# The order of the steady batches written anew in a fused attention and feed-forward kernel

## The chip, the cores and the metric

The kernel runs on one core of a Trainium2 chip. The metric is device time in microseconds (us) from one launch to its end; a time is the median of several runs, and beside it stands one profiled execution, from which all rows of the trace come.

## What is computed

For each of 8 batches and 8 heads (576 tokens, 64 columns), a softmax of phi over 32 memories weights the keys and values into 32 memory rows; the queries then attend to these rows, and the result goes through a gated feed-forward network.

```
a = softmax(phi, axis=2)                      # (b, h, s, m), m = 32
k_m = einsum('bhsm,bhsd->bhmd', a, k);  v_m = einsum('bhsm,bhsd->bhmd', a, v)
attn = softmax(q @ k_m^T / sqrt(64))          # (b, h, s, m)
x = (attn @ v_m) laid out as (4608, 512)
h = x @ w_in                                  # (4608, 2048)
out = (h * clip(h + 3, 0, 6) / 6) @ w_out     # (4608, 512)
```

## The kernel before, in words

The kernel never forms x. It folds the memory values into w_in (v_m @ w_in, a "fold", one for each quarter of w_in: fo, then two parts vh and vl that split it into a rounded high part and its remainder), so that h is the product of the probabilities and the folded weights. All large products are done three times, high x high, high x low and low x high, from pairs of rounded numbers: ACT casts the high part, DVE or POOL subtracts it for the remainder.

Batches 0 to 2 run from an order written out word by word (`BEGIN`, `THIRD`). Batches 3 to 7, the steady ones, are 160 steps, 32 to a batch; I call a step a row, as the texts do. Rows 0 to 15 are the first half of the batch's tokens (256), rows 16 to 31 the second (320). The second product of two rows is done in Strassen's way with seven blocks. A row does this, on each engine in the order of the program:

- PE: the first product of this row (`gemm1`, L716, 6 matmuls); then what the text puts into this row; then the second product of three rows before (`products`, L688, 9 or 12 matmuls). Some of its right sides are read from DRAM (`stream`, three loads of 256 KB every second row).
- ACT: `relu` (L722); the text's words; the high part of the blocks (L756).
- DVE: `gate` (L735, L739); in odd rows one addition of blocks (L745); the remainder of the blocks (L761), which in odd rows stands behind the text's words and in even rows ahead of them. A second product can't start without it; it has two rows' time.
- POOL: in odd rows the other sums of blocks (L749, L750). At the end of a half, in rows 2 and 18, DVE and POOL put the output together (L798 to L804) and SP stores it (L806).

In batches 4, 6 and at the end the leftover tokens of two batches are done first ("rest stage", `RestUnit`, L822 to L862): it lies in row 2, and the words of rows 0, 1 and 2 are played within it.

The texts `STEADY` and `EVERY` (with `FOURTH` in place of `STEADY` for batch 3) say in which row the attention of the next batch is done, word by word: C is the batch itself, N the next, M the one after. Words that the change moves:

- fo.C.3, vh, vl: the fourth fold and its two halves (0 and 1), L428, L439, L448.
- bh, bl: high part and remainder of the probabilities (half 0 or 1), L412 on ACT, L417 on POOL.
- sp: the spread, a DMA that brings the maxima of phi to all partitions (L288); xa and xe: subtraction on DVE (L306, L309) and exponential on ACT (L313).
- mem, nr, nk, tp, tk: the key and value products over the memories (L323, 80 matmuls), their division and turn.
- q, pt, pn, kv: loads of the queries, of phi in two layouts and of the keys with values (five tiles).
- sc, ct, cm, cs, ex, ds, dr, dm, bt: scores (L361), their transposition (L377), maximum (L387), subtraction on POOL (L391), exponential (L394), sum (L387), reciprocal (L399), division on POOL (L403), transposition back (L407).
- mx, mt, mo: maxima of phi, their transposition and store (L271, L277, L283).
- fetch.N.c.h: half h of quarter c of w_in from DRAM (L217).

The program keeps each engine's order as the texts issue it. All loads and stores go through SP's queue: a load whose buffer has not been given back, or a store whose source is not ready, waits at its head, and the rest behind it. Queries, phi, keys and values share five buffers of one kind; the quarters of w_in share two, and a load takes a free one.

Of the kernel before, what the change touches and what calls it, by code (L numbers as in the profile page):

```python
# [96 lines left out]
"""  # L97

STEADY = """
0 fo.C.3 vh.C.3.0 vl.C.3.0 / 3 vh.C.3.1 / 4 vl.C.3.1 bh.C.1 / 5 bl.C.1  # L100
"""

EVERY = """
0 sp.N / 5 fetch.N.0.0 / 6 xa.N.0 / 7 xe.N.0 fetch.N.0.1 / 8 xa.N.1 xa.N.2 / 9 xe.N.1 fetch.N.1.0 / 10 xe.N.2 / 11 mem.N fetch.N.1.1
/ 12 nr.N nk.N q.N.0 / 13 q.N.1 / 14 tp.N tk.N / 16 sc.N.0 ct.N.0 pt.M / 17 kv.M.0
/ 20 sc.N.1 ct.N.1 pn.M / 21 cm.N.0 cs.N.0 cm.N.1 kv.M.1 / 22 fo.N.0 vh.N.0.0 vl.N.0.0 / 23 fetch.N.2.0 vh.N.0.1 vl.N.0.1 ex.N.0 cs.N.1 fetch.N.2.1
/ 24 ds.N.0 dr.N.0 dm.N.0 mx.M.0 / 25 fo.N.1 vh.N.1.0 vl.N.1.0 ex.N.1 / 26 vh.N.1.1 vl.N.1.1 mx.M.1 fetch.N.3.0
/ 27 ds.N.1 dr.N.1 bt.N.0 dm.N.1 mt.M mo.M kv.M.2 / 28 fo.N.2 vh.N.2.0 vl.N.2.0 bh.N.0 / 29 vh.N.2.1 vl.N.2.1 bl.N.0 fetch.N.3.1
/ 30 bt.N.1 kv.M.3 / 31 kv.M.4
"""  # L110

CONVERT = (25, 29, 33, 37, 41, 45, 49, 53)
# [1012 lines left out]
```

## Time and profile before

| | |
|---|---|
| median of 3 runs | 705.71 us (704.71 to 706.06) |
| the profiled execution | 705.24 us, of which the span 703.2 |
| busy in the span | PE 680.7 us (97%), DVE 532.1 (76%), ACT 388.1 (55%), POOL 333.0 (47%) |
| DMA | 162.86 MB, mean 232 GB/s; one key tile 516.0 KB, one half quarter of w_in 512.0 KB, one stream load 256.0 KB |
| granted clock of TensorE | 0.998 of full speed |

The profile is of one execution. Times in its rows are in us from the start of the span; L numbers are lines of the kernel. Busy shares are averages: what a change is worth is read from the rows around it.

### The profile page before, as it was taken

Reading aid. Unit: us, or ns where it says so; the run is one execution under the profiler, and the core shown is the slowest. Engines: PE = TensorE matmul, PEld = TensorE weight load, DVE = VectorE, ACT = ScalarE, POOL = GpSimd, SP = SyncE. Lnnn points to the kernel's source line nnn. Section 1 sums busy time; section 2 is a strip of 40 time slices with the busy share of each in tenths; the row PEclk is TensorE's granted clock in tenths of the full one; section 3 lists DMA queues with packets and bytes.
Section 4 is the critical chain, followed back from the end, with each engine's and each line's share of the span. In section 5 each row is a group of like instructions: output and inputs, shape, how many; then the busy total and the mean of one; then the engine's idle time right before and its main releaser. Section 6 shows DMA issues by size and latency. Waiting matters only on the chain.

```text
span 703.2 us, 14752 instructions
## 1 busy us (share of the span) xinstructions
PE 680.7 (97%) x5622; PEld 577.2 (82%) x5622; DVE 532.1 (76%) x962; ACT 388.1 (55%) x786; POOL 333.0 (47%) x333
## 2 busy tenths in 40 slices
PE   8999999999999999999999999899999999999997
PEld 3456777878877787789889998799988999889997
DVE  4899987776466455566998869977898778987765
ACT  4677785554344455554655655555465555655543
POOL 2645330396564574632545435453457334554433
PEclk9999999999999999999999999999999999999999
DMA  9988573655671784899673877749675593736351
GB/s 353 421 328 314 181 270 125 225 178 178 270 260 47 277 291 132 302 375 343 221 260 118 265 273 271 275 166 332 216 262 191 155 323 114 270 118 219 121 180 47
DMA packets 66270, 162.86 MB, mean 232 GB/s; under 512 B 6808, under 2 KB 13976, under 8 KB 63640
## 3 DMA queue, kind: packets, MB, share of 16 engines
q1 hardware_dynamic: 66120, 161.86, 65.2%
q8 instruction: 44, 0.72, 0.4%
q14 instruction: 26, 0.21, 0.1%
q10 hardware_dynamic: 80, 0.07, 0.0%
HBM read 135.68 MB, written 26.22 MB: 230 GB/s over the span
## 4 chain that ended last, share of the span: by engine, by line
PE 47%; DVE 27%; DMA 9%; ACT 7%; issue 4%; POOL 3%; SPq 2%; ACTq 0%; POOLq 0%; DVEq 0%
PE acc L688 17%; PE acc L545 11%; PE ph L491 7%; PE ph L716 7%; DVE rounded L761 7%; DVE gated L735 3%; DVE gated L745 3%; DVE both L448 2%; DMA stream<-kept 2%; DMA w<-w_kept 2%; ACT rounded L756 2%; PE pk L323 2%; DMA kvt<-in_kv 2%; PE pv L428 2%; DMA kept<-stage 1%
## 5 line engine op out<-in xcount | busy, mean ns | idle before, releaser
L688 PE MATMUL acc<-w,rounded 128*128 128x256 f32 x1248 | 177.7, 282 | 4.4 <-DVE rounded L761 3.8
L688 PEld LDWEIGHTS acc<-w,rounded 128*128 128x128 f32 x1248 | 157.7, 188 | 26.7 <-issue 10.8
L749 POOL TENSOR_TENSOR gated<-gated 128x256 f32<-128x256 f32 x80 | 76.8, 961 | 189.0 <-DVE gated L735 158.2
L761 DVE TENSOR_TENSOR rounded<-gated,rounded 128x384 fp32r<-128x384 f32 (+1 forms) x160 | 133.2, 833 | 38.0 <-ACT rounded L756 32.5
L716 PE MATMUL ph<-probs,both 128*128 128x256 f32 (+1 forms) x960 | 150.4, 292 | 0.0
L756 ACT CAST rounded<-gated 128x384 fp32r<-128x384 f32 (+1 forms) x160 | 90.6, 567 | 95.3 <-DVE gated L745 89.2
L716 PEld LDWEIGHTS ph<-probs,both 128*128 128x128 f32 x960 | 131.6, 188 | 0.2
L722 ACT ACTIVATE gf<-ph,three 128x256 f32<-128x256 f32 (+1 forms) x160 | 79.9, 499 | 42.3 <-PE ph L716 40.7
L545 PE MATMUL acc<-w,ghi 128*128 128x512 f32 x384 | 101.0, 398 | 0.1
L688 PE MATMUL acc<-stream,rounded 128*128 128x256 f32 x720 | 97.3, 279 | 1.5 <-DMA stream<-kept 1.3
L688 PEld LDWEIGHTS acc<-stream,rounded 128*128 128x128 f32 x720 | 88.6, 188 | 3.6 <-DMA stream<-kept 2.5
L545 PEld LDWEIGHTS acc<-w,ghi 128*128 128x128 f32 x384 | 68.9, 188 | 23.9 <-issue 5.7
L735 DVE SCALAR_TENSOR_TENSOR gated<-gf,ph 128x256 f32<-128x256 f32 x160 | 65.5, 410 | 27.0 <-ACT gf L722 26.9
L491 PEld LDWEIGHTS ph<-probs,both 128*128 128x128 f32 x528 | 75.0, 188 | 11.2 <-DVE gf L507 5.2
L491 PE MATMUL ph<-probs,both 128*128 128x256 f32 (+1 forms) x528 | 78.5, 297 | 2.7 <-DVE gf L507 2.6
L507 DVE SCALAR_TENSOR_TENSOR gf<-gf,ph 128x576 f32<-128x576 f32 x44 | 33.0, 750 | 40.8 <-ACT gf L501 40.6
L501 ACT ACTIVATE gf<-ph,three 128x576 f32<-128x576 f32 (+2 forms) x52 | 36.5, 703 | 43.0 <-PE ph L491 38.1
L545 PE MATMUL acc<-w,glo 128*128 128x512 f32 x192 | 54.0, 390 | 0.0
L448 DVE TENSOR_TENSOR both<-pv,both 128x512 fp32r<-128x512 f32 x62 | 42.3, 682 | 14.9 <-ACT both L439 14.7
L525 DVE TENSOR_TENSOR glo<-gf,ghi 128x512 fp32r<-128x512 f32 x44 | 39.1, 892 | 12.8 <-PE acc L545 7.0
L439 ACT CAST both<-pv 128x512 fp32r<-128x512 f32 x62 | 36.1, 584 | 20.7 <-DVE both L448 13.6
L194 POOL TENSOR_TENSOR w<-tmp,raw 128x512 uint32<-128x512 uint32 x14 | 21.8, 1580 | 45.2 <-DVE tmp L184 24.5
(106 smaller groups left out, 886.9 us busy)
## 6 DMA issues: line engine op xcount, KB each, us to landing
stream<-kept SPq DMA_DIRECT2D x186, 256.0 KB, 4.4
kvt<-in_kv SPq DMA_DIRECT2D x32, 516.0 KB, 7.0
w<-w_kept SPq DMA_DIRECT2D x32, 512.0 KB, 6.0
raw<-in_w SPq DMA_DIRECT2D x16, 512.0 KB, 8.6
raw<-in_w SPq DMA_DIRECT2D x8, 1024.0 KB, 7.9
out_t<-o SPq DMA_DIRECT2D x16, 512.0 KB, 3.3
w<-w_kept SPq DMA_DIRECT2D x8, 1024.0 KB, 7.8
kept<-stage SPq DMA_DIRECT2D x24, 256.0 KB, 4.4
```

Of the source, the lines that this page charges most:

```text
L448: nc.vector.tensor_tensor(both[:, 1], src, both[:, 0].bitcast(F32), ALU.subtract)
L491: nc.tensor.matmul(dst, w[:, g, fs], x[:, g * n : (g + 1) * n], start=(i == 0), stop=(i == len(seq) - 1),)
L501: nc.scalar.activation(self.gf, self.h, AF.Relu, bias=three)
L525: nc.vector.tensor_tensor(self.glo[:, :n], self.gated(), self.ghi[:, :n].bitcast(F32), ALU.subtract)
L545: nc.tensor.matmul(accs[self.b, self.rest, k].rearrange("p (x c) -> p x c", c=VC), left[:, t * P : (t + 1) * P], w, start=k in self.first ...
L688: nc.tensor.matmul(dst, left[l], right[r], start=begin and n == 0, stop=end and n == 2, skip_group_check=True)
L716: nc.tensor.matmul(h, w[:, g, fs], x[:, g * self.n : (g + 1) * self.n], start=(i == 0), stop=(i == len(seq) - 1))
L722: nc.scalar.activation(self.gf, self.h[k], AF.Relu, bias=three)
L735: nc.vector.scalar_tensor_tensor(dst, by_tile(self.gf), 6.0, by_tile(self.h[k]), ALU.min, ALU.mult)
L749: nc.gpsimd.tensor_tensor(g[:, 2:4], g[:, 0::8], g[:, 1:8:6], ALU.subtract)
L756: nc.scalar.copy(self.parts[0][:, at], self.g[:, 1:8][:, at])
L761: nc.vector.tensor_tensor(low[:, at], self.g[:, 1:8][:, at], high[:, at].bitcast(F32), ALU.subtract)
```

## The change

Two texts are written anew; no function, tile or instruction is changed, and each word that was there is there once.

```
-STEADY: 0 fo.C.3 vh.C.3.0 vl.C.3.0 / 3 vh.C.3.1 / 4 vl.C.3.1 bh.C.1 / 5 bl.C.1
+STEADY: 1 fo.C.3 vh.C.3.0 vl.C.3.0 / 5 bh.C.1 / 7 vh.C.3.1 / 9 vl.C.3.1 / 12 bl.C.1
 EVERY:
-0 sp.N / 5 fetch.N.0.0 / 6 xa.N.0 / 7 xe.N.0 fetch.N.0.1 / 8 xa.N.1 xa.N.2 / 9 xe.N.1 fetch.N.1.0 / 10 xe.N.2 / 11 mem.N fetch.N.1.1
-/ 12 nr.N nk.N q.N.0 / 13 q.N.1 / 14 tp.N tk.N / 16 sc.N.0 ct.N.0 pt.M / 17 kv.M.0
-/ 20 sc.N.1 ct.N.1 pn.M / 21 cm.N.0 cs.N.0 cm.N.1 kv.M.1 / 22 fo.N.0 vh.N.0.0 vl.N.0.0 / 23 fetch.N.2.0 vh.N.0.1 vl.N.0.1 ex.N.0 cs.N.1 fetch.N.2.1
-/ 24 ds.N.0 dr.N.0 dm.N.0 mx.M.0 / 25 fo.N.1 vh.N.1.0 vl.N.1.0 ex.N.1 / 26 vh.N.1.1 vl.N.1.1 mx.M.1 fetch.N.3.0
-/ 27 ds.N.1 dr.N.1 bt.N.0 dm.N.1 mt.M mo.M kv.M.2 / 28 fo.N.2 vh.N.2.0 vl.N.2.0 bh.N.0 / 29 vh.N.2.1 vl.N.2.1 bl.N.0 fetch.N.3.1
-/ 30 bt.N.1 kv.M.3 / 31 kv.M.4
+3 sp.N / 5 fetch.N.1.0 / 6 xa.N.0 / 7 xa.N.2 fetch.N.0.0 / 8 xa.N.1 xe.N.0 fetch.N.0.1 / 9 xe.N.2 xe.N.1 q.N.0 / 11
+q.N.1 mem.N / 12 nr.N nk.N / 13 fetch.N.1.1 / 15 tp.N pt.M tk.N / 16 sc.N.0 ct.N.0 / 18 kv.M.0 / 19 sc.N.1 / 20 ct.N.1
+cm.N.0 / 21 cs.N.0 cm.N.1 / 22 pn.M fo.N.0 vh.N.0.0 vl.N.0.0 / 23 mx.M.0 fetch.N.2.0 vh.N.0.1 kv.M.1 vl.N.0.1 ex.N.0
+cs.N.1 ds.N.0 fetch.N.2.1 / 25 ex.N.1 fo.N.1 vh.N.1.0 dr.N.0 vl.N.1.0 dm.N.0 mx.M.1 / 26 vh.N.1.1 vl.N.1.1 bt.N.0
+fetch.N.3.0 / 27 ds.N.1 dr.N.1 mt.M bh.N.0 mo.M / 28 fo.N.2 vh.N.2.0 vl.N.2.0 / 29 bl.N.0 vh.N.2.1 vl.N.2.1
+fetch.N.3.1 kv.M.2 / 30 dm.N.1 / 31 kv.M.3 bt.N.1 kv.M.4
```

`FOURTH`, which holds batch 3's own words, is not changed.

## Rows read from the trace of the kernel before

**Rows 1.** Windows: from:to length, busy us (instructions) PE PEld DVE ACT POOL, clock, DMA.

```profile
641.46:645.20 3.74, 3.74 (x36) 3.74 (x34) 2.66 (x6) 1.98 (x4) 1.40 (x2) 1.00 0.69 214
...
624.42:629.73 5.31, 4.61 (x35) 4.01 (x34) 4.66 (x8) 2.58 (x6) 3.67 (x4) 1.00 0.33 103
391.36:399.21 7.85, 7.77 (x69) 7.58 (x68) 6.62 (x12) 4.50 (x9) 4.58 (x5) 1.00 0.95 288
467.82:476.44 8.62, 8.24 (x69) 7.84 (x67) 7.39 (x14) 4.70 (x10) 4.51 (x5) 1.00 0.91 320
629.73:637.72 7.99, 7.99 (x69) 7.70 (x67) 6.76 (x12) 4.07 (x9) 4.52 (x5) 1.00 0.72 243
609.68:611.58 1.90, 1.90 (x18) 1.90 (x16) 1.90 (x5) 0.86 (x2) 0.44 (x1) 1.00 0.70 210
522.87:525.36 2.49, 2.19 (x17) 2.00 (x16) 2.49 (x6) 1.52 (x3) 1.09 (x1) 1.00 0.32 27
529.59:533.92 4.33, 4.06 (x36) 3.87 (x34) 3.75 (x9) 2.25 (x6) 2.75 (x4) 1.00 0.97 346
371.76:385.92 14.16, 14.16 (x133) 13.20 (x131) 12.16 (x24) 7.03 (x22) 7.79 (x11) 1.00 0.23 75
533.92:549.91 15.99, 15.41 (x132) 13.84 (x131) 12.12 (x24) 7.18 (x22) 7.78 (x11) 1.00 0.23 76
```

**Rows 2.** Timeline of PE, row 0 of batch 5 and row 2 of batch 6.

```profile
454.72 1.09 PE L428 MATMUL pv<-w,kvT 64*32 64x512 f32 x16 [1.64 <-DMA w<-w_kept]
...
535.68 1.64 PE L688 MATMUL acc<-stream,rounded 128*128 128x256 f32 x7 [0.58 <-DMA stream<-kept]
```

**Rows 3.** Timeline of DVE in batch 5: start, us, instruction.

```profile
464.16 1.29 DVE L745 TENSOR_TENSOR gated<-gated 128x256 f32<-128x256 f32 x1
...
470.93 1.71 DVE L761 TENSOR_TENSOR rounded<-gated,rounded 128x512 fp32r<-128x512 f32 x1
...
511.73 0.66 DVE L761 TENSOR_TENSOR rounded<-gated,rounded 128x384 fp32r<-128x384 f32 x1 [0.19 <-ACT rounded L756]
...
513.99 0.67 DVE L387 TENSOR_REDUCE sm<-st 128x16 f32<-128x512 f32 x1
...
523.17 1.21 DVE L761 TENSOR_TENSOR rounded<-gated,rounded 128x384 fp32r<-128x384 f32 x1
...
528.65 1.32 DVE L761 TENSOR_TENSOR rounded<-gated,rounded 128x512 fp32r<-128x512 f32 x1
```

**Rows 4.** Timeline of POOL in batch 5.

```profile
463.88 1.29 POOL L804 TENSOR_TENSOR o<-o 128x512 f32<-128x512 f32 x1 [0.25 <-DVE o L799]
...
470.20 1.88 POOL L417 TENSOR_TENSOR probs<-pT,probs 128x640 fp32r<-128x640 f32 x1
...
511.94 1.58 POOL L391 TENSOR_TENSOR st<-st,mx 128x640 f32<-128x640 f32 x1
...
522.70 1.27 POOL L403 TENSOR_TENSOR st<-st,sm 128x640 f32<-128x640 f32 x1 [0.49 <-DVE sm L399]
...
527.81 1.61 POOL L417 TENSOR_TENSOR probs<-pT,probs 128x512 fp32r<-128x512 f32 x1
```

**Rows 5.** Timeline of PE in batch 5, rows 11, 14 and 25.

```profile
479.25 2.35 PE L323 MATMUL pk<-kvt,pnat 128*32 128x129 f32 x80
...
487.67 1.23 PE L688 MATMUL acc<-stream,rounded 128*128 128x256 f32 x9
...
514.14 1.30 PE L688 MATMUL acc<-w,rounded 128*128 128x256 f32 x9
```

**Rows 6.** Waits of DVE, 290 us to the end: total, times, longest us.

```profile
DVE rounded L761 <- ACT rounded L756: 32.5, 59, 0.6
```

**Rows 7.** Timeline of SP's queue, batch 5.

```profile
465.19 0.39 SPq L806 DMA_DIRECT2D out_t<-o  x1
```

**Rows 8.** The spread's tile: landing of its loads.

```profile
DMA to landing us min/median/max: 3.9/4.4/5.4
```

**Rows 9.** The streams' tile, 290 us to the end: landing of its loads.

```profile
DMA to landing us min/median/max: 2.5/4.4/8.8
```

More of the change, by code (lines that the diff above doesn't have):

```diff
@@ L99 @@
 STEADY = """
-0 fo.C.3 vh.C.3.0 vl.C.3.0 / 3 vh.C.3.1 / 4 vl.C.3.1 bh.C.1 / 5 bl.C.1
+1 fo.C.3 vh.C.3.0 vl.C.3.0 / 5 bh.C.1 / 7 vh.C.3.1 / 9 vl.C.3.1 / 12 bl.C.1
 """
 EVERY = """
-0 sp.N / 5 fetch.N.0.0 / 6 xa.N.0 / 7 xe.N.0 fetch.N.0.1 / 8 xa.N.1 xa.N.2 / 9 xe.N.1 fetch.N.1.0 / 10 xe.N.2 / 11 mem.N fetch.N.1.1
-/ 12 nr.N nk.N q.N.0 / 13 q.N.1 / 14 tp.N tk.N / 16 sc.N.0 ct.N.0 pt.M / 17 kv.M.0
-/ 20 sc.N.1 ct.N.1 pn.M / 21 cm.N.0 cs.N.0 cm.N.1 kv.M.1 / 22 fo.N.0 vh.N.0.0 vl.N.0.0 / 23 fetch.N.2.0 vh.N.0.1 vl.N.0.1 ex.N.0 cs.N.1 fetch.N.2.1
-/ 24 ds.N.0 dr.N.0 dm.N.0 mx.M.0 / 25 fo.N.1 vh.N.1.0 vl.N.1.0 ex.N.1 / 26 vh.N.1.1 vl.N.1.1 mx.M.1 fetch.N.3.0
-/ 27 ds.N.1 dr.N.1 bt.N.0 dm.N.1 mt.M mo.M kv.M.2 / 28 fo.N.2 vh.N.2.0 vl.N.2.0 bh.N.0 / 29 vh.N.2.1 vl.N.2.1 bl.N.0 fetch.N.3.1
-/ 30 bt.N.1 kv.M.3 / 31 kv.M.4
+3 sp.N / 5 fetch.N.1.0 / 6 xa.N.0 / 7 xa.N.2 fetch.N.0.0 / 8 xa.N.1 xe.N.0 fetch.N.0.1 / 9 xe.N.2 xe.N.1 q.N.0 / 11
[4 more added lines that the diff above has]
+fetch.N.3.1 kv.M.2 / 30 dm.N.1 / 31 kv.M.3 bt.N.1 kv.M.4
 """
```

## The prediction

> **What bounds the kernel now.** Three views, in this order. The page's busy shares (table above) have PE at 97%, DVE at 76%, POOL at 47%: PE sets the time, and only its waits can be won. Next I cut the steady part into stretches that start and end with the first matmul of a row's first product. Two undisturbed rows of a first half take 3.74 us, PE busy throughout; the same matmuls elsewhere take longer, and the excess is what a new order can win or lose [rows 1]:
> - rows 6 to 9: 8.62 us in batch 5, 7.99 in batch 7, 7.85 in batch 4 (batch 6 alike, so two), against 2 x 3.74 = 7.48: 1.14 + 0.51 + 2 x 0.37 = 2.39 us;
> - row 29: 2.49 us in batches 3 to 5 (three alike), 1.90 in batch 6, which has no maxima left: 3 x 0.59 = 1.77;
> - rows 0 and 1 ahead of the rest stage: 4.33 against 3.74 (two alike): 1.18;
> - row 2 with the rest stage: 15.99 in batch 6, 14.16 in batch 4: 1.83;
> - rows 4 and 5 of batch 7 (batch 5 nearly alike): 5.31, so 1.57 each.
>
> Last, the timelines of PE, DVE and POOL say what each excess waits for. In batch 5's row 0 the fourth fold stands 1.64 us for its weights' DMA; in batch 6 the stage's products stand for a stream's [rows 2]. The others end on a DVE remainder (L761) that came late, and beside each late one POOL works: 1.71 us from 470.93 beside the probabilities' remainder from 470.20, 1.21 from 523.17 beside a division, 1.32 from 528.65 beside the first half's remainder [rows 3, 4].
>
> **Fold from row 0 to 1, key loads later.** One row later is about half of 3.74 us, above the 1.64 us wait; besides, the third key load (516 KB, 1.5 us at the 346 GB/s of a full stretch [rows 1]) now queues behind the last half of the weights. The wait goes: **-1.64**. What is late next: the fold's first remainder on DVE now comes in row 1, before that row's own. It has the fold's time on PE (1.09 us [rows 2]) as cover; uncovered it would be a remainder's length, 0.66 us in the nearest form [rows 3].
>
> **Second half's probabilities (row 5 to 12), second part of the fourth fold (3 and 4 to 7 and 9).** In rows 4 to 6 DVE loses a remainder of the fold and the 1.15 us from 470.93 to POOL's end at 472.08 for which it stood [rows 3, 4]: more than the 1.14 of batch 5's excess. POOL's 1.9 us now fall into rows 11 and 12, where the key products hold PE for 2.35 us [rows 5], so DVE is ahead. The fold's remainder in row 9 and the short maxima in row 7 stand in odd rows between two steps where DVE waits for ACT anyway (32.5 us in 59 waits, 0.6 at most [rows 6]). I take 2.1 of the 2.39: **-2.1**. If the cover failed, the same 1.14 would come back some rows on. Rows 4 and 5 stay: there the addition of 464.16 takes 1.29 us beside POOL's last sum of the output from 463.88, and neither is moved [rows 3, 4].
>
> **Divisions.** The second goes from row 27 to 30, the turn of the first from 27 to 26. In row 27 the remainder of 523.17 loses its POOL neighbour (1.21 us; the same form takes 0.66 at 511.73) and a transpose ahead of it, against an excess of 0.59: **-1.77** in three batches. In row 30 the second division (1.27 us) stands right behind the first half's remainder (1.61 us from 527.81 [rows 4]) and ends near 530.7; the turn behind it, now in row 31, finds DVE's gap behind ACT. Rows 0 and 1 gain nearly all: **-1.0** of 1.18.
>
> **Key loads and the rest stage.** The fourth load goes past row 30's three stream loads, so these land 1.5 us sooner; batch 6 stood for them [rows 2]. I take **-1.5** of 1.83. The keys are next needed eleven rows later.
>
> **Row 23.** It takes in a maximum and the first half's sums (0.67 us each). The remainder, now at 511.73, starts 1.3 us later, inside POOL's subtraction (1.58 us from 511.94, so to 513.52), and ends behind it near 514.0; PE asks for it at 514.14 [rows 3 to 5]. Row 24 is emptied in return and DVE is level in row 25. Bounds: 0, and 4 batches x 0.9 us if the sums are held up too. Nearest to the row is a graze: **+0.8**. The Trainium skill (SBUF — State Buffer, "SBUF: two separate sides") says that GpSimd and a DVE instruction with two SBUF inputs, or in a mode with two ports, exclude each other for a whole instruction. By it the sums, with one input, would not be held, and this term would be near 0; no row here shows a reduction beside such a POOL instruction.
>
> **Rows 15 to 21** (turn of the keys, second scores, maximum in row 20): the same instructions, one row apart, PE's work between them unchanged: 0, bounds +-0.5.
>
> **Spread from row 0 to 3.** It now queues on SP behind the output's store (issued at 465.19 in batch 5) and so leaves at 465.6; at its longest landing, 5.4 us, it is there at 471.0. Its first reader on DVE stands behind the remainder of 470.93, which without the stretch ends near 471.5 [rows 3, 7, 8]. Hidden, with 0.5 us to spare; in batch 3, among crowded loads, I allow **+0.3**. In batches 4 and 6 it follows the stage's stores with three rows left.
>
> **SP queue.** The query's first load moves from row 12 to 9, ahead of the key products of row 11 whose buffer it takes, and holds the queue until their first fifth is done: 479.25 + 0.5. Row 10's three streams then go out from 480.2 to 481.5; row 14 reads them from 487.67 [rows 5]. At the median landing of 4.4 us [rows 9]: 0. The two weight chunks change places; the third goes into whichever buffer is free, and chunk 0's is. 0.
>
> **Sum.** -1.64 - 2.1 - 1.77 - 1.0 - 1.5 = -8.0; +0.8 + 0.3, and +0.4 for new meetings of POOL and DVE, make +1.5. Net -6.5. From the profiled execution's 705.24 that is 698.7; the median shown is 0.5 above it, so I forecast **699.0**. Its own range: all excess but rows 4 and 5 gone (1.64 + 2.39 + 1.77 + 1.18 + 1.83 = 8.8) gives 696.5; half of the gain gives 702.
>
> **Rivals.**
> - POOL back to back holds DVE. In row 30 remainder and division follow without a gap; if DVE gets in only behind both, its remainder ends 1.3 us later than counted, and row 23 costs its 0.9: about 1.0 us more in each of four batches, 703. For it: every stretched row ends after its POOL neighbour. Against: 0.3 to 0.6 us after it and no more (465.45 after 465.17, 529.97 after 529.42 [rows 3, 4]).
> - The SP queue decides, slower than before. The longest stream landing is 8.8 us [rows 9]: from 480.2 + 0.4 the first is there at 489.4, 1.7 us after 487.67, and the restart costs some 0.5: 2.2 x 4 = 8.8, so 699.0 + 8.8 = 707.8. It decides from landings over 6.5 us. For it: a 512 KB load goes out just ahead. Against: the median; and the key loads that crowd rows 27 to 31 are not queued here.
> - Nothing won: DVE's total is the same, so every lateness only moves to the next rows, 705.5. For it: DVE is at 0.86 of batch 5's rows 6 to 9. Against: batch 6's row 29, which has all but the maxima and no excess [rows 1].
> - The change doesn't do what it says in one place: the spread lands after 471.5. 1 us in each of four batches gives 703; counted with the first.
>
> **How the numbers follow.** Forecast 0.70; first and last rival together 0.14; nothing won 0.09; SP queue 0.07. A difference under 0.2% (1.4 us) can't be told from none here. Faster: 0.70 + 0.12 = 0.82; same: 0.02 + 0.08 = 0.10; slower: 0.07 + 0.01 = 0.08. The range reaches from 695.8, where rows 4 and 5 give a little too, to 704.0, which takes in the first rival and leaves out the last two.
>
> **What would show it.** Right: row 0 of batch 5 without a DMA wait in front of the fold; rows 6 to 9 near 7.5 us in batches 4 to 7; row 29 at 1.9; batch 6's stage near 14.2; rows 4 and 5 still above 5. Wrong: L761 over 1 us in rows 23 to 25 or 30 with PE waiting behind it; the spread's reader on DVE standing for a DMA; PE waiting for streams in row 14. The prediction falls if rows 20 to 31 of a batch are longer than before.

## The result, and the profile after

The changed kernel takes 696.13 us (median of 4 runs, 695.33 to 696.87), the kernel before 705.88 (4 runs, 704.71 to 706.07): a ratio of 0.9868, 95% interval 0.9852 to 0.9883. The forecast was 699.0, its range 695.8 to 704.0: the median fell by 9.75 us where 6.7 was forecast, which is near the fast end of the range. The profiled execution takes 696.87 us, 8.4 less than before's; its span went from 703.2 to 695.1, and this 8.1 us is what the rows below divide up.

The page after: busy time by engine, the chain of waits by engine, and one group (line, engine, form, count, then busy us, mean ns of one, idle time before it and what ended it).

```profile
PE 676.9 (97%) x5618; PEld 575.2 (83%) x5622; DVE 529.0 (76%) x962; ACT 389.0 (56%) x786; POOL 335.7 (48%) x333
...
PE 73%; DMA 8%; DVE 8%; ACT 4%; POOL 3%; issue 2%; SPq 2%; ACTq 0%; POOLq 0%; DVEq 0%
...
L761 DVE TENSOR_TENSOR rounded<-gated,rounded 128x384 fp32r<-128x384 f32 (+1 forms) x160 | 123.5, 773 | 27.2 <-ACT rounded L756 24.2
```

And before, the chain and the same group:

```profile
PE 47%; DVE 27%; DMA 9%; ACT 7%; issue 4%; POOL 3%; SPq 2%; ACTq 0%; POOLq 0%; DVEq 0%
...
L761 DVE TENSOR_TENSOR rounded<-gated,rounded 128x384 fp32r<-128x384 f32 (+1 forms) x160 | 133.2, 833 | 38.0 <-ACT rounded L756 32.5
```

The busy shares hardly moved. What moved is the chain: PE's part of it is 73%, where it was 47%, and DVE's 8%, where it was 27%. A remainder (L761) takes 773 ns in the mean, where it took 833: 160 of them are 9.7 us less of DVE.

The same stretches as in [rows 1], after the change: batch 5 rows 0 and 1, then 4 and 5; rows 6 to 9 of batches 4 and 5; row 29 of batch 5; batch 4 rows 0 and 1; row 2 with the rest stage in batches 4 and 6; batch 3 rows 4 and 5, then 6 to 9; batch 6 rows 14 and 15.

```profile
451.60:456.57 4.97, 4.97 (x52) 4.01 (x50) 4.68 (x10) 2.95 (x7) 3.13 (x5) 1.00 1.02 385
...
460.31:464.70 4.39, 4.03 (x36) 3.83 (x35) 3.77 (x7) 2.24 (x5) 2.85 (x4) 1.00 0.38 127
...
391.70:399.18 7.48, 7.48 (x69) 7.48 (x68) 6.79 (x14) 5.51 (x12) 2.85 (x4) 1.00 0.99 332
464.70:472.18 7.48, 7.48 (x69) 7.48 (x68) 6.75 (x14) 5.30 (x12) 2.79 (x4) 1.00 0.98 314
...
518.58:520.47 1.89, 1.89 (x18) 1.89 (x16) 1.89 (x6) 0.98 (x3) 0.00 (x0) 1.00 0.20 49
366.97:370.71 3.74, 3.74 (x36) 3.74 (x34) 3.74 (x8) 2.45 (x7) 3.74 (x5) 1.00 1.00 363
...
370.71:386.26 15.55, 15.20 (x133) 13.63 (x132) 11.79 (x24) 6.92 (x21) 7.59 (x11) 1.00 0.26 98
528.34:543.20 14.86, 14.83 (x133) 13.55 (x132) 12.01 (x24) 6.88 (x21) 7.76 (x11) 1.00 0.26 100
298.74:303.71 4.97, 4.97 (x51) 4.01 (x50) 2.71 (x7) 2.47 (x5) 1.39 (x2) 1.00 1.04 358
303.71:314.55 10.84, 9.34 (x69) 8.11 (x67) 7.68 (x16) 5.14 (x11) 2.83 (x4) 1.00 0.95 337
566.09:571.09 5.00, 4.85 (x38) 4.26 (x36) 3.12 (x7) 2.45 (x6) 1.39 (x3) 1.00 0.90 318
```

And before, the stretches that now matter too: batch 5 rows 0 and 1; batch 3 rows 4 and 5, then 6 to 9; batch 6 rows 14 and 15.

```profile
452.25:458.93 6.68, 5.04 (x52) 4.04 (x51) 4.68 (x10) 2.55 (x5) 1.32 (x2) 1.00 0.85 309
...
298.75:305.61 6.86, 6.03 (x52) 4.36 (x51) 2.52 (x7) 2.46 (x5) 1.39 (x2) 1.00 1.06 400
305.61:314.33 8.72, 8.32 (x69) 7.71 (x68) 7.68 (x15) 5.16 (x11) 2.78 (x4) 1.00 0.99 351
573.23:577.27 4.04, 4.04 (x37) 4.04 (x36) 2.92 (x6) 2.45 (x6) 1.40 (x2) 1.00 0.94 307
```

Differences in the table are taken before rounding.

| term, us in the profiled execution | forecast | measured | from |
|---|---|---|---|
| fold's wait, batch 5 | -1.64 | -1.71 | rows 0 and 1, 6.68 to 4.97 |
| rows 6 to 9 of four batches | -2.1 | -2.38 | all 7.48 |
| row 29 of three batches | -1.77 | -1.77 | all near 1.89 |
| rows 0 and 1 ahead of the stage | -1.0 | -1.28 | 4.44 and 4.33 to 3.74 |
| rest stage, batches 4 and 6 | **-1.5** | **+0.26** | +1.39 and -1.13 |
| row 23 of four batches | +0.8 | 0 | rows 22 to 28 of batches 3 to 6 are 18.31 before and after |
| spread, batch 3 | +0.3 | +0.23 | rows 4 and 5 -1.89, rows 6 to 9 +2.12 |
| new meetings of POOL and DVE | +0.4 | 0 | no row that took one in is longer |
| rows 4 and 5, batches 5 and 7 | 0 | -1.67 | 5.15 to 4.39, 5.31 to 4.40 |
| row 14, batch 6 | 0 | +0.96 | 4.04 to 5.00 |
| rest | 0 | -0.7 | 0.38 in batch 7's rows 22 to 28; the others under 0.1 a row, where rows that only trade time with the next one (19 and 20) are counted together |

The 0.38 is not the change's: that stretch takes 14.99 us before and in experiments 5 and 8 below, 14.61 in the changed kernel and in experiments 1 to 4.

Each kernel has one profile, and the variants below tell which rows repeat. The fold's rows, rows 4 and 5, rows 6 to 9 of batches 4 to 7 and row 29 come out within 0.05 us of the table in experiments 5 to 8 too. The rest stage, rows 4 to 9 of batch 3 and row 14 do not. Batch 6's stage takes 15.99 us before and 14.67 in experiment 2, whose edit doesn't touch it; rows 4 to 9 of batch 3 take 15.57, 14.92, 15.03, 15.14 and 14.65 before and in experiments 1 to 4, with the same words. In these places a difference of under 1 us between two profiles is not told from none.

### The profile page after: what moved, and what is told of

It is laid out like the page before. It is cut to its first block, busy times and chain, and to the rows that moved or that the text cites. A ratio compares the mean times of both kernels' runs of the same rounds, so it can differ in the third digit from the quotient of the medians.

```text
span 695.1 us, 14709 instructions
## 1 busy us (share of the span) xinstructions
PE 676.9 (97%) x5618; PEld 575.2 (83%) x5622; DVE 529.0 (76%) x962; ACT 389.0 (56%) x786; POOL 335.7 (48%) x333
## 4 chain that ended last, share of the span: by engine, by line
PE 73%; DMA 8%; DVE 8%; ACT 4%; POOL 3%; issue 2%; SPq 2%; ACTq 0%; POOLq 0%; DVEq 0%
PE acc L688 30%; PE ph L716 16%; PE acc L545 12%; PE ph L491 7%; PE pv L428 4%; DMA stream<-kept 3%; PE pk L323 2%; DMA kvt<-in_kv 2%; DMA w<-w_kept 1%; DMA kept<-stage 1%; DVE gf L507 1%; PE psc L361 1%; PE acc L872 1%; DMA out_t<-o 1%; DVE glo L525 1%
## 5 line engine op out<-in xcount | busy, mean ns | idle before, releaser
L688 PE MATMUL acc<-w,rounded 128*128 128x256 f32 x1248 | 173.8, 280 | 1.5 <-DVE rounded L761 1.5
L761 DVE TENSOR_TENSOR rounded<-gated,rounded 128x384 fp32r<-128x384 f32 (+1 forms) x160 | 123.5, 773 | 27.2 <-ACT rounded L756 24.2
```

Source lines behind the costliest of these rows:

```text
L688: nc.tensor.matmul(dst, left[l], right[r], start=begin and n == 0, stop=end and n == 2, skip_group_check=True)
L761: nc.vector.tensor_tensor(low[:, at], self.g[:, 1:8][:, at], high[:, at].bitcast(F32), ALU.subtract)
```

## The experiments

Each time stands beside runs of the kernel before on the same chip. Lengths are of the profiled execution, cut at the first products as above.

**1. The fold alone** (kernel before, first part of the fourth fold one row later).

```
-0 fo.C.3 vh.C.3.0 vl.C.3.0 / 3 vh.C.3.1
+1 fo.C.3 vh.C.3.0 vl.C.3.0 / 3 vh.C.3.1
```

> The kernel before with one thing done: the fourth fold and its first half go from row 0 to row 1. Theory (fold in row 1 gives ACT time): the 1.64 us wait in batch 5's row 0 goes, and the fold's PE time in row 1 lets ACT's scaling of the output (leave_first) end before row 2's relu, so DVE is about 0.8 us earlier and rows 4 and 5 fall from 5.15 and 5.31 us to about 4.4 in batches 5 and 7: in all 1.7 + 1.7 = 3.4, so about 702.4. Rival (words taken out of rows 3 to 5 are what made them short): rows 4 and 5 stay at 5.2, only 1.7 us won, about 704.1.

700.55 us against 706.09, ratio 0.9925 (0.9904 to 0.9946). Its windows of batch 5 rows 0 and 1, then 4 and 5:

```profile
451.74:457.12 5.38, 5.05 (x51) 4.04 (x50) 4.77 (x11) 2.60 (x6) 1.88 (x3) 1.00 0.98 347
460.86:465.25 4.39, 4.02 (x36) 3.83 (x34) 3.77 (x7) 2.43 (x6) 2.85 (x4) 1.00 0.41 125
```

The row alone takes 1.30 of the fold's 1.71 us; its products still stand 0.33 us for the weights in row 1. And rows 4 and 5, which the forecast left as they were, shorten by 0.76 in batch 5 and 0.60 in batch 7 with nothing but the fold moved. The timeline of ACT shows why. Before, batch 5, and in this experiment:

```profile
460.01 0.59 ACT L789 ACTIVATE o<-acc 128x512 f32<-128x512 f32 x1
...
460.76 0.48 ACT L722 ACTIVATE gf<-ph,three 128x256 f32<-128x256 f32 x1
```

```profile
457.40 0.59 ACT L789 ACTIVATE o<-acc 128x512 f32<-128x512 f32 x1
...
458.16 0.47 ACT L722 ACTIVATE gf<-ph,three 128x256 f32<-128x256 f32 x1
```

Row 2's products start at 458.93 before and at 457.12 here. ACT's two output copies (L789, and L790 behind it) used to start 1.08 us after that and to hold row 2's relu back to 1.83 us behind it. With the fold between row 1's two products, PE comes to row 2 later, and ACT's copies start 0.28 us behind it, the relu 1.04 us (0.94 in the changed kernel). The output's sums, which rows 4 and 5 meet, come sooner with it.

The median is 1.9 us better than the 702.4 expected. The three places give 2.7 of the span's 4.2 us; most of the rest lies in rows that the edit doesn't touch, 0.65 in batch 3's rows 4 to 9, 0.38 in batch 7's rows 22 to 28 and 0.40 ahead of batch 3.

**2. The remainder and the fold's second part** (kernel before, the rest of `STEADY` as changed, first part of the fold left in row 0).

```
-0 fo.C.3 vh.C.3.0 vl.C.3.0 / 3 vh.C.3.1 / 4 vl.C.3.1 bh.C.1 / 5 bl.C.1
+0 fo.C.3 vh.C.3.0 vl.C.3.0 / 5 bh.C.1 / 7 vh.C.3.1 / 9 vl.C.3.1 / 12 bl.C.1
```

> The kernel before with the other words of STEADY alone: cast of the second half's probabilities in row 5, the fold's second half in rows 7 and 9, the remainder on POOL in row 12. Theory: rows 6 to 9 fall from 8.62, 7.99 and 2 x 7.85 us to 7.48 (2.4 us in all), rows 4 and 5 stay at 5.2 to 5.3, about 703.4. Rival: rows 4 and 5 fall to about 4.4 as well, 1.7 us more, about 701.7.

701.83 us, ratio 0.9941 (0.9921 to 0.9961). Batch 5 rows 4 and 5, then 6 to 9:

```profile
461.90:467.08 5.18, 4.59 (x36) 4.00 (x34) 4.53 (x8) 2.24 (x5) 3.54 (x4) 1.00 0.34 107
...
467.08:474.56 7.48, 7.48 (x69) 7.48 (x67) 6.25 (x12) 5.23 (x11) 2.73 (x4) 1.00 1.01 359
```

Rows 6 to 9 are 7.48 in batches 4 to 7 by this alone, and rows 4 and 5 stay at 5.18 and 5.29. So the two halves of `STEADY` are told apart: rows 6 to 9 belong to these four words, rows 4 and 5 to the fold's row. The remainder that took 1.71 us beside POOL [rows 3] takes 0.69 at the same place:

```profile
469.56 0.69 DVE L761 TENSOR_TENSOR rounded<-gated,rounded 128x512 fp32r<-128x512 f32 x1
```

But the fold's second remainder on DVE also left these rows, and no run moves POOL's remainder by itself. The median is 1.6 us below the 703.4 expected and near the rival's 701.7, which the rows refute: of the span's 4.6 us, 2.4 are rows 6 to 9, and 1.3 batch 6's rest stage, which the edit doesn't touch.

**3. The second division alone** (kernel before; row 27 to 30, its turn to 31).

```
-27 ds.N.1 dr.N.1 bt.N.0 dm.N.1 mt.M mo.M kv.M.2   / 30 bt.N.1 kv.M.3 / 31 kv.M.4
+27 ds.N.1 dr.N.1 bt.N.0 mt.M mo.M kv.M.2          / 30 dm.N.1 kv.M.3 / 31 bt.N.1 kv.M.4
```

> The kernel before with the second division alone moved from row 27 to 30, and the transposition back behind it from row 30 to 31; the first half's transposition stays in row 27. Theory (the POOL neighbour): row 27's remainder falls from 1.21 to about 0.85 us, row 29 from 2.49 to 1.9 in batches 3 to 5, rows 0 and 1 ahead of the rest stage from 4.33 and 4.43 to 3.8: 3 us before the stage; of it batch 4's stage gives 1 back, since its streams come no earlier: about 704. Rival (the transposition ahead of it is what made row 27 late): row 29 stays above 2.2, and less than 1 us is won in all.

704.85 us (10 runs, 703.24 to 708.58), ratio 0.999 (0.9971 to 1.0009): no difference. Its windows of batch 5 row 29, batch 4 rows 0 and 1, and a piece of the latter; its remainder of row 27 on DVE; and its PE in batch 4 row 0 and batch 5 row 0:

```profile
525.16:527.05 1.89, 1.89 (x17) 1.89 (x16) 1.89 (x7) 1.51 (x3) 0.00 (x0) 1.00 0.02 5
366.33:374.20 7.87, 5.62 (x36) 5.42 (x34) 5.79 (x13) 3.14 (x9) 4.84 (x6) 0.78 0.80 278
...
370.45:372.50 2.05, 2.05 (x9) 2.05 (x10) 0.85 (x3) 0.00 (x0) 0.37 (x1) 0.50 0.94 364
```

```profile
525.45 0.52 DVE L761 TENSOR_TENSOR rounded<-gated,rounded 128x384 fp32r<-128x384 f32 x1
```

```profile
370.45 1.01 PE L688 MATMUL acc<-stream,rounded 128*128 128x256 f32 x3 [2.25 <-DMA stream<-kept]
...
457.04 1.09 PE L428 MATMUL pv<-w,kvT 64*32 64x512 f32 x16 [2.07 <-DMA w<-w_kept]
```

The mechanism is confirmed: without the division beside it the remainder takes 0.52 us where it took 1.21 [rows 3], with the first division's turn still ahead of it, and row 29 is 1.89 in all three batches. But nothing is won. PE comes to the crowded loads of rows 30 to 1 sooner by these 0.6 us and stands there: 2.07 us for the weights in batch 5 (1.64 before [rows 2]), 2.25 us for a stream in batch 4, where it stood for none before. The first grew by 0.43 us, no more than PE came sooner. The second is longer than that: its load went out at 363.15 and landed 7.3 us later, the one in its place before went out at 363.56 and landed after 5.2. Why it took longer is not shown; experiment 1 comes to batch 4 as early (366.31, here 366.33), and its rows 0 and 1 take 4.45 us. Behind the stand in batch 4 the granted clock was 0.50 for 2.05 us, the lower level of 1.2 GHz, and 0.61 for 1.70 more, so this stretch loses a second time.

**4. The key loads alone** (kernel before, rows of three of the five loads).

```
-21 ... kv.M.1 / 27 ... kv.M.2 / 29 ... fetch.N.3.1 / 30 bt.N.1 kv.M.3 / 31 kv.M.4
+23 ... kv.M.1 ... / 29 ... fetch.N.3.1 kv.M.2 / 30 bt.N.1 / 31 kv.M.3 kv.M.4
```

> The kernel before with the key loads alone moved: the second to row 23, the third behind the last weights' load in row 29, the fourth to row 31. Theory (streams queue behind keys): batch 6's row 2 falls from 15.99 to about 14.5 us, batch 4's stays at 14.16, and the fold's wait in batch 5's row 0 shrinks from 1.64 to under 0.5: about 2.5 us, 703.2. Rival (the loads in front of the streams are no limit): both stay as they are, 705.7.

703.04 us (10 runs, 700.97 to 706.57), ratio 0.9964 (0.9943 to 0.9985). PE in batch 5 row 0 and in batch 6 row 2:

```profile
453.93 1.09 PE L428 MATMUL pv<-w,kvT 64*32 64x512 f32 x16 [1.37 <-DMA w<-w_kept]
...
534.74 1.88 PE L688 MATMUL acc<-stream,rounded 128*128 128x256 f32 x9 [0.38 <-DMA stream<-kept]
```

Both waits are still there: 1.37 us where it was 1.64, 0.38 where it was 0.58; row 2 of batch 6 is 15.39 instead of 15.99. Of the 1.5 us that the forecast gave to these moves, 0.6 came in this profile, less than this stage differs by between profiles. The median is near the 703.2 expected, but not for the reason expected: of the span's 1.9 us, 0.9 lies in batch 3's rows 4 to 9, whose words the edit leaves alone.

**5. The changed kernel, spread back in row 0.**

```
-3 sp.N / 5 fetch.N.1.0
+0 sp.N / 5 fetch.N.1.0
```

> The changed kernel with the spread alone back in row 0. Theory (the spread in row 3 is not what row 8 of batch 3 stands for; streams are): batch 3's row 8 gets shorter by about the time by which rows 4 to 6 get longer, since the placed streams' store queues behind the spread again; batches 4 to 6 unchanged; the time within 0.7 us of the changed kernel's. Rival (DVE's 3 us at the spread's reader is the cause): batch 3's rows 4 to 9 get 2 us shorter, about 694.

694.99 us against 704.72, ratio 0.9873 (0.9841 to 0.9904). Batch 3 rows 4 and 5, then 6 to 9:

```profile
299.02:305.95 6.93, 6.01 (x52) 4.33 (x50) 2.51 (x7) 2.46 (x5) 1.38 (x2) 1.00 1.04 392
305.95:314.70 8.75, 8.33 (x68) 7.74 (x67) 8.21 (x16) 5.28 (x11) 2.83 (x4) 1.00 1.03 383
```

15.68 us in all, as before (15.58) and after (15.81): the spread's row says in which rows batch 3 pays for its crowded loads. Whether it also changes how much can't be read from differences as small as these.

**6. The changed kernel, query loads back in rows 12 and 13.**

```
-9 ... q.N.0 / 11 q.N.1 mem.N / 12 nr.N nk.N / 13 fetch.N.1.1
+9 ... / 11 mem.N / 12 nr.N nk.N q.N.0 / 13 q.N.1 fetch.N.1.1
```

> The changed kernel with the query loads back in rows 12 and 13, behind the key products. Theory (the query's load at the head of SP's queue delays row 10's streams): batch 6's row 14 falls from 3.02 to 2.04 us, the other batches unchanged: 1 us, about 695.1. Rival (the streams of row 14 are late by the amount of loads, whatever the order): row 14 stays near 3, time unchanged.

694.89 us, ratio 0.9864 (0.984 to 0.9888). Batch 6 rows 14 and 15:

```profile
564.77:568.78 4.01, 4.01 (x37) 4.01 (x36) 3.12 (x7) 2.45 (x6) 1.42 (x3) 1.00 1.00 288
```

The loss of 0.99 us is gone, but that is not shown to be the edit's doing: rows 14 and 15 take 4.01 us in experiments 5, 7 and 8 too, where the query loads stand as in the changed kernel. What the edit does show is when row 10's three streams go out: 1.55 us behind the row's first product here (556.35 after 554.80), 3.90 in the changed kernel (560.02 after 556.12) and in experiments 5, 7 and 8. In those three they landed 5.3 to 6.4 us after they went out, in the changed kernel's profile 7.3 to 7.6, and only there PE stood for them.

**7. The changed kernel, key loads back in rows 21, 27 and 30.**

```
-23 ... kv.M.1 ... / 29 ... fetch.N.3.1 kv.M.2 / 30 dm.N.1 / 31 kv.M.3 bt.N.1 kv.M.4
+21 ... kv.M.1 / 27 ... kv.M.2 / 29 ... fetch.N.3.1 / 30 dm.N.1 kv.M.3 / 31 bt.N.1 kv.M.4
```

> The changed kernel with the second to fourth key loads back in rows 21, 27 and 30. Theory (they queue ahead of row 30's streams): row 2 gets about 1.5 us longer in batches 4 and 6 (15.55 and 14.86 now), about 699. Rival: the stage's length is set by when PE arrives and by the total of loads, so both stay, about 696.

696.25 us, ratio 0.9886 (0.986 to 0.9911). Row 2 of batches 4 and 6:

```profile
371.12:386.24 15.12, 15.12 (x132) 13.78 (x131) 11.15 (x22) 6.75 (x20) 7.46 (x10) 1.00 0.17 65
528.41:543.51 15.10, 15.02 (x133) 13.44 (x131) 11.94 (x24) 6.82 (x21) 7.57 (x11) 1.00 0.24 89
```

30.22 us against 30.41 with the loads moved (30.09 and 29.60 in experiments 5 and 6, which move them too): the change's rows for the keys do nothing for the rest stage that these profiles could show.

**8. The changed kernel, third key load in row 31, behind the streams.**

```
-29 ... fetch.N.3.1 kv.M.2 / 30 dm.N.1 / 31 kv.M.3 bt.N.1 kv.M.4
+29 ... fetch.N.3.1 / 30 dm.N.1 / 31 kv.M.2 kv.M.3 bt.N.1 kv.M.4
```

> The changed kernel with the third key load alone moved from row 29 to row 31, behind row 30's streams. Theory (the prediction missed that the third load took the fourth's place ahead of these streams): with no key load between the weights and the streams, row 2 is 14.15 us in batches 4 and 6 (15.55 and 14.86 now), 2.1 us in all, and batch 6's row 14 keeps its 1 us: about 694. Rival (the three streams are late by the weights ahead of them): row 2 stays above 14.7.

694.62 us against 707.37, ratio 0.9823 (0.9808 to 0.9839). Row 2 of batch 4:

```profile
370.71:384.86 14.15, 14.15 (x132) 13.19 (x131) 11.96 (x24) 6.93 (x21) 7.70 (x11) 1.00 0.27 102
```

14.15 in batch 6 too: one word, and the whole stage is as long as its matmuls, here and in both batches of experiments 9 and 10. The interval ends below the changed kernel's (from 0.9852), though the two did not run side by side. Batch 6's rows 14 and 15 took 4.01 as well, with the query loads untouched; that I had not expected.

**9. and 10. The best of these together, and batch 3's loads of the second weights later.** The ninth is the changed kernel with 6, 8 and, in `FOURTH`, the load rp.7 in row 8 instead of 3. The tenth is the ninth with rp.6 in row 7 instead of 0 and rp.7 in row 9.

> The changed kernel with three things more: query loads back in rows 12 and 13, the third key load behind row 30's streams too (row 31), and batch 3's last replacement of weights (rp.7) from row 3 to row 8, behind the streams of rows 4 to 6. Theory (loads ahead of streams): batch 6's row 14 1 us shorter, row 2 of batches 4 and 6 shorter by up to 1.4 and 0.7, batch 3's row 8 by about 0.7: about 693. Rival (the stretches are limited by the total of loads): within 1 us of the changed kernel.

> The fastest kernel so far (queries in rows 12 and 13, third key load in row 31, rp.7 in row 8) with rp.6 moved from row 0 to 7 and rp.7 to 9 in batch 3. Theory (loads ahead of streams and of the stores that DVE waits for): rows 4 to 9 of batch 3 fall from 14.55 us by another 0.7 to 1.5, about 691.5. Rival (these rows are limited by the stores themselves): unchanged, 692.6.

The ninth takes 692.61 us (692.48 to 693.22) against 704.72, ratio 0.9834 (0.9806 to 0.9862). Each of its 4 runs is below each of the sixth's (694.49 to 695.36) on the same chip. Its row 2 is 14.15 in both batches, batch 6's rows 14 and 15 take 4.01, and batch 3's rows 4 to 9 take 14.55 instead of 15.81, hardly less than experiment 4 had without a move there (14.65). The tenth's profile has 13.43 there, less than any other, yet its time, 693.04 us against 707.37, ratio 0.9809 (0.9786 to 0.9832), is not to be told from the ninth's. Both beat the kernel before. The changed kernel itself did not run beside them: the sixth differs from it by the query loads alone, and of the ratios the tenth's interval ends below the changed kernel's (from 0.9852), while the ninth's reaches a little into it.

## Why the prediction was right, and where not

That the time fell inside the range is in part luck. The terms came out 1.6 us beyond the forecast's sum, with misses on both sides: the rest stage and row 14 brought 2.7 us less than forecast, and rows 4 and 5, row 23, the meetings that cost nothing and several smaller terms 4.3 more. The sum itself slips by 0.2: 705.7 less 6.5 is 699.2. Of the signs of being wrong two came, each once: PE stood for streams in row 14 of batch 6, and the spread's reader for its load in batch 3. Of the signs of being right two failed: rows 4 and 5 are not above 5 us, and batch 6's stage is 14.86 and not near 14.2.

**Right, with its mechanism: the stretched remainders.** Rows 6 to 9, row 29, and rows 0 and 1 ahead of the stage make -5.43 of the 8.1 us, forecast -4.87. Experiment 3 gives row 29 to the POOL neighbour that the forecast named, experiment 2 rows 6 to 9 to the words of which its other neighbour is one. For rows 0 and 1 the cause stays open: the remainder that the forecast named there takes 1.32 us as before (528.65 in [rows 3], and the row from 450.00 below), yet PE no longer stands for DVE. Experiment 3, with the division gone from row 27, leaves batch 6's rows 0 and 1 at 4.21.

**Right in size, half right in cause: the fold.** The row did 1.30 of the 1.71 (experiment 1). That the weights come sooner gave 0.27 alone (experiment 4).

**Failed: "The fourth load goes past row 30's three stream loads, so these land 1.5 us sooner".** The timelines of SP's queue ahead of batch 4 show the step that I left out. Before; after; and experiment 8:

```profile
363.94 0.42 SPq L217 DMA_DIRECT2D w<-w_kept  x1
364.40 0.43 SPq L238 DMA_DIRECT2D kvt<-in_kv  x1
364.95 1.37 SPq L684 DMA_DIRECT2D stream<-kept  x3
```

```profile
363.51 0.34 SPq L238 DMA_DIRECT2D kvt<-in_kv  x1
364.59 2.52 SPq L684 DMA_DIRECT2D stream<-kept  x3
367.16 1.48 SPq L238 DMA_DIRECT2D kvt<-in_kv  x1
```

```profile
364.59 1.27 SPq L684 DMA_DIRECT2D stream<-kept  x3
365.91 1.96 SPq L238 DMA_DIRECT2D kvt<-in_kv  x2
```

One key tile stands ahead of the streams before and after. The fourth did go behind them, but the change also moved the third load from row 27, where it had landed 2.0 us ahead of row 0, to row 29: it took the fourth's place. I priced the load that left and not the one that came. The last of the three streams landed at 373.29 before, and in the changed kernel PE's weight load that waits for it starts at 373.47: not sooner at all. The first went out at 364.59 in the changed kernel and in experiment 8; it landed at 372.19 in the one, and in the other the second was there at 370.31. Besides, in batch 4 row 2 begins 1.05 us sooner, so PE now meets the same streams before they land: that batch, which had no wait, got 1.39 us, and batch 6 kept 0.71 of its 1.83. Experiment 7 finds no difference between the old rows of the key loads and the new ones; experiments 8 to 10 show that the step holds once both loads stand behind, in six stages of six.

**Failed the other way: "Rows 4 and 5 stay".** I argued that the addition of 464.16 keeps its POOL neighbour. It does, 1.29 us as before:

```profile
461.01 1.29 DVE L745 TENSOR_TENSOR gated<-gated 128x256 f32<-128x256 f32 x1
```

But I didn't ask when it starts. It now comes 0.70 us behind row 4's first product (460.31), where it came 1.49 behind it before (464.16 after 462.67), because ACT's copies hold row 2's relu back less (experiment 1). That is worth 1.67 us in the two batches.

**Mis-sized: row 23, +0.8, costs nothing.** DVE and POOL there, batch 5:

```profile
507.84 0.67 DVE L387 TENSOR_REDUCE sm<-st 128x16 f32<-128x512 f32 x1
508.44 0.88 DVE L761 TENSOR_TENSOR rounded<-gated,rounded 128x384 fp32r<-128x384 f32 x1
```

```profile
507.65 1.26 POOL L391 TENSOR_TENSOR st<-st,mx 128x640 f32<-128x640 f32 x1
```

The sums lie wholly inside POOL's subtraction and take the 0.67 us of [rows 3]. The remainder behind them enters with 0.47 of the subtraction left, ends 0.41 after it, and PE asks 0.52 later, at 509.84. The rule of the Trainium skill that spoke against my +0.8 (SBUF — State Buffer, "SBUF: two separate sides") agrees with this trace: a reduction with one input was not held, a subtraction with two was (0.88 us, where it took 0.66 in [rows 3]).

**The rivals.** POOL back to back does not hold DVE. In row 30 of batch 4 POOL's remainder and division follow without a gap, and DVE's remainder, begun at 450.00, ends at 451.32, 0.55 us behind POOL's first and well within its second. It is POOL's division that takes longer: 1.71 us, and 1.71 to 1.72 in the other batches, where it took 1.27 [rows 4].

```profile
450.00 1.32 DVE L761 TENSOR_TENSOR rounded<-gated,rounded 128x512 fp32r<-128x512 f32 x1
```

```profile
449.16 1.61 POOL L417 TENSOR_TENSOR probs<-pT,probs 128x512 fp32r<-128x512 f32 x1
450.74 1.71 POOL L403 TENSOR_TENSOR st<-st,sm 128x640 f32<-128x640 f32 x1
```

The SP queue showed in one batch of four: in batch 6 the query's load went out at 559.64, the three streams from 560.02, and these landed at 567.4 to 568.6, over 7 us later. It cost 0.96 us where I allowed 2.2 in each of four batches, and it needs landings as long as these, which experiments 5, 7 and 8 do not have with the same query loads. The 0.5 us for a restart in its price stands in no run: behind the 1.64 us before, batch 5's rows 0 and 1 took 1.71 more than the changed kernel's 4.97, behind the 2.07 of experiment 3 2.15 more. The longest landing of a stream is 8.4 us, the median 4.8. "Nothing won" describes experiment 3, the division alone. The four parts alone come to 0.75 + 0.59 + 0.10 + 0.36 = 1.80% less, the change to 1.32%; with intervals of 0.2 on either side of each part, that difference is hardly clear of noise, and whether any of it is given back in the crowded loads stays open.

**The late spread** came true in batch 3 alone: its loads land in 4.6 to 7.0 us where they took 3.9 to 5.4 [rows 8], and once DVE stood for one, while PE stood for a stream anyway, until 310.99:

```profile
310.30 0.69 DVE L309 TENSOR_TENSOR pnat<-pnat,nmxb 128x512 f32<-128x512 f32 x1 [3.05 <-DMA nmxb<-nmx]
```

## What to carry to other kernels

When a load is moved behind others, write down the whole queue before and after: what took its place ahead of them counts as much as what left. What PE gains ahead of a stretch with crowded loads can be lost there, as in experiment 3; look for the next load it will meet before counting the gain. And an operation that goes to another row moves everything queued behind it on each engine: ask what now runs first, not only what it no longer meets. And before a difference in one profile is given to an edit, look at the same rows in runs that left them alone.

## What the runs showed of the hardware that was not expected

- A wait of PE cost more than its length once: behind 2.25 us for a stream the granted clock was 0.50 for 2.05 us (experiment 3, batch 4). Behind the 2.07 us for the weights in the same run it stayed at 1.00 in the 4.2 us from 457.04.
- DVE got in between two POOL operations that follow without a gap: its remainder ended 0.55 us after the first, inside the second, and the second took 1.71 us instead of 1.27.
- A load of 256 KB on the one queue took 2.5 to 8.4 us to land after the change. The same three loads of batch 6's row 10, issued at the same point behind the row's first product, took 7.3 to 7.6 us in one kernel's profile and 5.3 to 6.4 in three others'.
